# Twenty-four sums move from two vector engines to accumulating DMAs, the rounding of the angles moves to ScalarE, and the order of all steps is written anew

## The chip, the cores and the metric

The kernel runs on one core of one Trainium2 chip. The metric is the device time of one execution in microseconds (us), the median over several executions. The profile is one execution of its own, recorded by the hardware profiler.

## The reference

Three stages follow each other, with B = 4 batches, S = 768 tokens, H = 8 heads of D = 48, and so 384 channels. All inputs are fp32 on the host, but the weights arrive as float64 and are converted in the kernel.

```python
# 1. attention with a decaying state, per batch and head, over tokens t
state = alpha[t, :, None] * state + outer(k[t], v[t]);  y[t] = q[t] @ state
# 2. first block: token mixing of rank 32, then a two-layer MLP of width 1536
u  = x + (x.T @ U @ V).T;      x1 = u + relu(u @ w_ch1) @ w_ch2
# 3. second block
theta = x1 @ w_theta           # 384 x 384
zr, zi = x1 * cos(theta), x1 * sin(theta)
y = w_tok_r @ zr + w_tok_i @ zi   # 768 x 768 each, over tokens
u = x1 + y;                    out = u + relu(u @ w_ch)
```

## The kernel before, in words

Tensors lie with 128 partitions. Every large fp32 product is made from three passes of a reduced fp32 type (fp32r): each factor is split into a high part (a cast on ScalarE, L161) and a low part (source minus high part, L162, on VectorE or GpSimd), and TensorE adds hi·hi, hi·lo and lo·hi. TensorE (PE in the profile) therefore does the same number of multiplications whatever the order; VectorE (DVE), ScalarE (ACT) and GpSimd (POOL) prepare its factors.

The attention (its helpers stand at L192 to L315) scans decays on DVE (`G` L200, `al` L209), scales keys and queries on DVE or POOL (`kk` L202, `qq` L210) and multiplies on PE. The first block follows: matmuls `h` and `acc` (L545 to L547), with L566, L567 and L587 to empty their banks. `x1` is spilled to DRAM (`x1d`) and read back later into `xq`, into which the result of the mixing is added.

The second block works in 24 **theta steps**, one for a batch b and a token chunk s of 128: nine matmuls into a PSUM bank `th`, three transposes of `x1` into a bank `x1t` (L705); ACT copies `x1t` to SBUF as `xc` (L719) and so frees the bank; DVE adds and subtracts a large constant to round the angle (L721, L722); ACT takes the absolute value and two sines (L725 to L727); DVE multiplies both by `xc` (L731, twice). The results of batches 0 and 1 lie side by side in `ZR[0, s]` and `ZI[0, s]`, those of batches 2 and 3 in `ZR[1, s]` and `ZI[1, s]`, each 128x768.

The mixing treats `w_tok_r`, `w_tok_i` and the z of two halves as a product of 2x2 blocks and makes it from seven products (the order is `TERMS`) instead of eight, each summed over six chunks s. For each of the 42 pairs (product, chunk), `factors` forms sums of weights (`cv`, 128x384) and of z (128x768), all at L773, in place, and splits both factors; `products7` then issues 18 matmuls `mx` (L818), and at a product's end DVE adds the banks into `xq` (L823, L825). The split of a z waits for ACT's high part, and PE waits for both parts. `operands` splits the final u, `outputs` makes the last matmuls `ch`.

Nothing is scheduled at run time. A string `ORDER` of 876 letters gives the order in which all the generators are advanced (H is a piece of a theta step, V a half of a factor pair, G six matmuls of a product), and so the order in each engine's queue. Tables of letters (`BY_T` for the splits of weights, `BY_Z` for those of z, `BY_S` for the sums, and others) say of each operation whether it runs on POOL (P) or DVE (V). SBUF slots and the eight PSUM banks are handed out from lists, first in, first out; a step that takes a bank waits until its last reader is done. DMAs are issued from SP (SyncE).

Of the kernel before, what the change touches and what calls it, by code (L numbers as in the profile page):

```python
# [37 lines left out]
APAQPAAABUUBUBBABAUBAPBPUUABAAALAA0A0UDPP0LB0LBBAP0BB0BB1B1PAL1A2LA1L2LAA221LAL22LL1LAMLLLLMNMLLMLMNNMMLLQMMUL  # L38
MNLLNNAUQLMDML1LNLLLMNNQMNLQLLUMNLLNLNLPLMMDMPNPQMMMMMPMANABBABDBNBABQBPDABAPAABBBQBPBNBBBPNANKLKNLKADAPKKAKQP
DKLANNKKPNNKBAKDAKBBBBMABMBBPTMAMQMAPMMQPMAMM1MMKMABAMBDBLPBMQAAMBAKBBBPDKMMPAMMKMPMLKKAMMKABBABAQUAKAKQBBTDTK  # L40
NANKPLDNNNNBTLPUNKNLNLNNBAPAPBNANKN2BTNTQBKFANBKNANNKQPABBNBBBTMAKNNNKKNMNMKMKNAMMMMKMKKUTMKMAQKNMTNKKNLMKMMNX
NNNM0NNNMKTMNNNMNNNMHNMTNMHMKNNMMKMMMHHNNTHHMKMMFHFMMHMMLMNMMMHKMMHMMMHMHXTNNHMHNMHTMHTHHTTHNNVTTHTTNTNNTHXNHN
# [6 lines left out]
BY_K = "PPPPPPVPVVPPPPVP"  # L49
BY_Q = "VVPPVPPPVPVPVVVP"  # L50
BY_W = "PPPPPPPVPPPP"
BY_A = "AAAAVVAAVVAAAAVAAAVAVAAVAVVVAVVV"
BY_Z = "PPPPVVPPPPPPPPPPPPPPPPVPPPPPPVVPVPVVPVPPPP"
# [13 lines left out]
def linear_attention_moe_kernel(ctx, tc, aT, kT, qT, vP, vT, U, V4, w1, w2, wth, wtr, wti, wch, out):  # L67
# [57 lines left out]
    def two(t):  # L125
        return t.rearrange("p (a b) -> p a b", a=2)
# [12 lines left out]
    halfpi = cst.tile([128, 1], F32, name="halfpi")  # L139
    ones = cst.tile([128, 1], F32, name="ones")  # L140
# [487 lines left out]
    def load_second(whole):  # L628
# [58 lines left out]
    def theta(b):  # L687
        for hf in range(2):
# [7 lines left out]
            for q in range(3):  # L696
# [13 lines left out]
                n, xc = two(T("nn")), T("xc")[:, 0:DM]  # L710
# [15 lines left out]
                act.activation(zi, n[:, 0], ACTF.Sin, scale=NEG2PI)  # L726
                act.activation(zr, n[:, 1], ACTF.Sin, scale=NEG2PI, bias=halfpi)  # L727
# [39 lines left out]

    def factors():
# [6 lines left out]
        for p in TERMS:  # L775
            for s in range(NC):
# [5 lines left out]
                ws, w, zs, z = term(p, s)  # L782
                add(ws)
# [7 lines left out]
                WP[p, s], ZP[p, s] = t, (zh, zl)  # L791
                if p == 7:
                    done_with(ZR[1, s])
                elif p == 5:
                    done_with(ZR[0, s], WT["r", s])
                elif p == 3:
                    done_with(ZI[1, s])
                elif p == 4:
                    done_with(ZI[0, s], WT["i", s])
                yield  # L800

    def products7():
        for p in TERMS:
            for s in range(NC):
# [5 lines left out]
                for j in range(KD):  # L810
                    c = slice(j * 128, (j + 1) * 128)
                    for q in range(2):
# [391 lines left out]
```

## Time and profile before

| | |
|---|---|
| runs | 711.95, 712.21, 714.93 us; median 712.21 |
| the profiled execution | 713.35 us, its span 711.6 us |
| mean granted TensorE clock | 0.978 of full speed |
| attention and first block | to about 482 us |
| second block, while angles and factors are made | about 482 to 639 us |
| remaining products and outputs | about 639 us to the end |

The page gives busy time by engine and cuts the span into slices. Of the trace three views matter here: busy time by stretch, the chain of waits (the work that ended last, followed back), and single instructions in order of time, which show what an operation takes alone and what it takes beside another engine's.

### The profile page before, as it was taken

How to read it: one execution, taken by the hardware profiler on the slowest of the kernel's cores; microseconds unless marked ns; L12 is line 12 of the kernel's file. 1: busy time of each engine (PE TensorE's matmuls, PEld its weight loads, DVE VectorE, ACT ScalarE, POOL GpSimd, SP SyncE). 2: the span in 40 equal slices, each digit the busy share in tenths (PEclk: the TensorE clock that was granted, in tenths of full speed). 3: DMA queues.
4: the chain of work that ended last, by engine and by line, in shares of the span. 5: the costliest groups of instructions: out<-in, count | busy, mean ns of one | idle time of the engine just before them, and what ended most of it. 6: DMA issues, size and time to landing. Idle time of an engine off the chain costs nothing.

```text
span 711.6 us, 11654 instructions
## 1 busy us (share of the span) xinstructions
PE 663.9 (93%) x4658; PEld 629.5 (88%) x4658; DVE 488.1 (69%) x689; ACT 278.6 (39%) x575; POOL 240.2 (34%) x185
## 2 busy tenths in 40 slices
PE   4879999999999999999999999999897887979996
PEld 3758899888999899999999999999797876979996
DVE  8878868668556667434235438988989989984742
ACT  3444453455433534322124334445654333331410
POOL 6642326424131023000000100214567778853700
PEclk9989999999999999999999999999998999899998
DMA  8523474445423412131000102634100114002102
GB/s 318 201 93 117 168 234 147 148 115 189 165 85 117 139 46 62 35 121 57 8 39 5 63 31 83 241 134 178 45 1 1 28 62 133 1 1 77 68 23 104
DMA packets 27966, 69.10 MB, mean 97 GB/s; under 512 B 3328, under 2 KB 10368, under 8 KB 27904
## 3 DMA queue, kind: packets, MB, share of 16 engines
q1 hardware_dynamic: 27904, 68.29, 28.6%
q8 instruction: 38, 0.62, 0.3%
q14 instruction: 24, 0.20, 0.1%
HBM read 54.12 MB, written 9.44 MB: 89 GB/s over the span
## 4 chain that ended last, share of the span: by engine, by line
PE 66%; DVE 25%; issue 3%; ACT 2%; POOL 2%; DMA 1%; DVEq 0%; ACTq 0%
PE acc L545 7%; PE acc L546 7%; PE acc L547 7%; PE h L545 7%; PE h L547 6%; PE h L546 6%; PE mx L818 5%; DVE zr L773 4%; PE A L255 4%; DVE cv L773 3%; PE Y L307 2%; PE Y L315 2%; DVE xq L825 2%; PE ch L547 2%; PE ch L546 2%
## 5 line engine op out<-in xcount | busy, mean ns | idle before, releaser
L818 PE MATMUL mx<-wp,zh 128*128 128x384 f32 x504 | 135.2, 350 | 9.6 <-DVE xq L825 5.0
L567 DVE SCALAR_TENSOR_TENSOR hh<-h,hh 128x384 fp32r<-128x384 f32 x96 | 52.7, 555 | 99.4 <-ACT hh L566 99.3
L818 PEld LDWEIGHTS mx<-wp,zh 128*128 128x128 f32 x504 | 94.2, 197 | 12.0 <-ACT zh L161 3.9
L545 PE MATMUL h<-uh,wh 128*128 128x384 f32 x288 | 98.5, 342 | 1.6 <-DVE hh L567 1.6
L545 PE MATMUL acc<-hh,wh 128*128 128x384 f32 x288 | 98.4, 342 | 0.0
L546 PE MATMUL acc<-hh,wh 128*128 128x384 f32 x288 | 96.4, 335 | 1.8 <-DVE hh L567 1.8
L547 PE MATMUL h<-uh,wl 128*128 128x384 f32 x288 | 96.5, 335 | 0.0
L547 PE MATMUL acc<-hh,wl 128*128 128x384 f32 x288 | 96.5, 335 | 0.0
L546 PE MATMUL h<-uh,wh 128*128 128x384 f32 x288 | 96.4, 335 | 0.0
L818 PE MATMUL mx<-wp,zl 128*128 128x384 f32 x252 | 88.5, 351 | 7.0 <-POOL zl L162 7.0
L566 ACT ACTIVATE hh<-h 128x384 fp32r<-128x384 f32 x96 | 46.1, 490 | 101.6 <-PE h L547 98.3
L162 POOL TENSOR_TENSOR wp<-cv,wp 128x384 fp32r<-128x384 f32 x33 | 44.0, 1339 | 76.8 <-DVE zr L731 40.2
L818 PEld LDWEIGHTS mx<-wp,zl 128*128 128x128 f32 x252 | 49.8, 198 | 9.7 <-POOL zl L162 9.5
L545 PEld LDWEIGHTS h<-uh,wh 128*128 128x128 f32 x288 | 54.1, 188 | 3.5 <-DVE hh L567 2.0
L546 PEld LDWEIGHTS acc<-hh,wh 128*128 128x128 f32 x288 | 54.1, 188 | 2.0 <-DVE hh L567 2.0
L545 PEld LDWEIGHTS acc<-hh,wh 128*128 128x128 f32 x288 | 54.1, 188 | 1.2 <-ACT hh L566 0.3
L546 PEld LDWEIGHTS h<-uh,wh 128*128 128x128 f32 x288 | 54.1, 188 | 0.0
L547 PEld LDWEIGHTS acc<-hh,wl 128*128 128x128 f32 x288 | 54.1, 188 | 0.0
L547 PEld LDWEIGHTS h<-uh,wl 128*128 128x128 f32 x288 | 54.1, 188 | 0.0
L162 POOL TENSOR_TENSOR zl<-zr,zh 128x768 fp32r<-128x768 f32 x22 | 44.8, 2039 | 15.1 <-ACT zh L161 14.8
L162 POOL TENSOR_TENSOR x1s<-Y,x1s 128x384 fp32r<-128x384 f32 x9 | 11.1, 1250 | 114.4 <-ACT x1s L161 114.4
L202 POOL TENSOR_TENSOR kk<-kk,G 128x767 f32<-128x767 f32 (+1 forms) x13 | 23.2, 1787 | 52.5 <-DVE G L200 34.4
(145 smaller groups left out, 1344.9 us busy)
## 6 DMA issues: line engine op xcount, KB each, us to landing
raw<-in_w SPq DMA_DIRECT2D x12, 768.0 KB, 4.4
al<-in_aT SPq DMA_DIRECT2D x15, 384.0 KB, 3.6
kk<-in_kT SPq DMA_DIRECT2D x15, 384.0 KB, 4.2
qq<-in_qT SPq DMA_DIRECT2D x15, 384.0 KB, 5.1
vv<-in_vP SPq DMA_DIRECT2D x16, 291.0 KB, 5.5
x1d<-X SPq DMA_DIRECT2D x12, 384.0 KB, 2.9
raw<-in_wti SPq DMA_DIRECT2D x6, 768.0 KB, 4.3
raw<-in_wtr SPq DMA_DIRECT2D x6, 768.0 KB, 4.2
```

The lines of the kernel that those rows point to most:

```text
L162: (e_lo or dve).tensor_tensor(out=lo, in0=src, in1=hi.bitcast(F32), op=ALU.subtract)
L202: (dve if BY_K[b * NP + p] == "V" else pool).tensor_tensor(out=k[:, x:y - 1], in0=k[:, x:y - 1], in1=G[:, x:y - 1], op=ALU.mult)
L255: pe.matmul(ts[h][:, j * C:(j + 1) * C], k[r, c], q[r, c], start=True, stop=True)
L307: pe.matmul(t[64 * h:64 * h + n, o], v[:, c * 96 + h * D:c * 96 + h * D + n], ms[g][h][:, j], start=(j == 0), stop=(c == 0), skip_group_ch ...
L315: pe.matmul(t[64 * h:64 * h + D, o], st[64 * h:64 * h + 64, :, c - 1], q[64 * h:64 * h + 64, c * C:(c + 1) * C], start=False, stop=True, s ...
L545: pe.matmul(out, a[0], b[0], start=first, stop=False)
L546: pe.matmul(out, a[0], b[1], start=False, stop=False)
L547: pe.matmul(out, a[1], b[0], start=False, stop=last)
L566: act.activation(h[:, 0], t[:, 0:HT], ACTF.Relu)
L567: dve.scalar_tensor_tensor(out=h[:, 1], in0=t[:, 0:HT], scalar=0.0, in1=h[:, 0].bitcast(F32), op0=ALU.max, op1=ALU.subtract)
L773: (dve if next(sums) == "V" else pool).tensor_tensor(out=o, in0=x, in1=y, op=op)
L818: pe.matmul(t[:, 0:HT], x[:, q, c], w[:, y], start=f, stop=l, skip_group_check=True)
```

## The change

What it does:

- 24 of the sums of `factors` become DMAs that add their source to what lies at their destination, SBUF to SBUF, issued from POOL (`plus`). Six add the i weights' half to the r weights' (128x384, as each r weight is converted); six add `ZI[1, s]` to `ZR[1, s]` (called a here; issued when the last batch's theta step of s is written); six add that result to `ZR[0, s]` (b; `later`, after product 1's factor is split, behind a); six add `ZR[0, s]` to `ZI[0, s]` (c; after product 6's split). The signs that the other sums need come from the sines' scale and bias; product 2 is then subtracted, not added.
- The rounding's first addition goes from DVE to ACT (Identity with a bias, 24 times).
- ACT's copy of `x1t` goes (24 times). DVE's two multiplications read the PSUM bank, which is kept until they are done.
- `ORDER` and the tables are new.

Instructions in the second block up to the last weight's split (before: from the trace, 482 to 639 us; after: counted in the order of the same stretch):

| | before | after |
|---|---|---|
| DVE, two operands in SBUF, 128x384 | 57 | 40 |
| DVE, two operands in SBUF, 128x768 | 39 | 28 |
| POOL, two operands in SBUF, 128x384 | 36 | 28 |
| POOL, two operands in SBUF, 128x768 | 29 | 21 |
| POOL, accumulating DMAs | 0 | 24 |
| DVE, one operand in PSUM (`xq`, rounding, multiplications) | 58 | 69 |

TensorE's instructions are the same in number and kind; their order differs.

```diff
 ORDER = """
-APAQPAAABUUBUBBABAUBAPBPUUABAAALAA0A0UDPP0LB0LBBAP0BB0BB1B1P
...
+APQAAAPAUUBBUUBBBAAAPPBUBUUAPABAA0LD0AAAPL0BL0BABPBB00BB11PB
...
-BY_T = "PVPVPVVPVPPPPPPPPPVPPPPPPPPPPPPVPPPPPPPVPV"
-BY_S = "PVPVVVPVVVVPVVVVVVVVVVVVVVVVVVVVVVVVVPVVVVVVVVVV"
...
+BY_T = "PPPVPPPPPPVVVPVVVPVPPPVPPPPPVPVVVPVVPVVPPV"
+BY_S = "VVVVVVVVVVVVVVVVVVVVVVVVPVVVVPPVVPPVVVVPPPVVPPPP"
...
+        pool.memset(minus, -HALFPI)
+        pool.memset(magic, MAGIC)
...
-                    WT[key] = two(v)
+                    WT[key] = w = two(v)
+                    if key[0] == "r":
+                        plus(w[:, 1], WT["i", key[1]][:, 1])
...
-                n, xc = two(T("nn")), T("xc")[:, 0:DM]
+                n, xc = two(T("nn")), xt[:, 0:DM]
...
-                act.copy(xc, xt[:, 0:DM])
-                done_with(xt)
-                dve.tensor_scalar(out=n[:, 0], in0=th[:, 0:DM], scalar1=MAGIC, scalar2=None, op0=ALU.add)
+                act.activation(n[:, 0], th[:, 0:DM], ACTF.Identity, bias=magic)
...
-                act.activation(zi, n[:, 0], ACTF.Sin, scale=NEG2PI)
-                act.activation(zr, n[:, 1], ACTF.Sin, scale=NEG2PI, bias=halfpi)
+                act.activation(zi, n[:, 0], ACTF.Sin, scale=NEG2PI if b in (2, 3, "any") else -NEG2PI)
+                act.activation(zr, n[:, 1], ACTF.Sin, scale=-NEG2PI if b in (2, 3) else NEG2PI,
+                               bias=minus if b in (2, 3) else halfpi)
...
-                done_with(xc)
+                done_with(xt)
                 if b in range(B):
                     made.add((b, s))
+                    if b == B - 1:
+                        plus(ZR[1, s], ZI[1, s])
...
     def term(p, s):
-            1: ([(wr1, wr1, add, wi1)], wr0, [], b11),
-            6: ([(wr0, wr1, sub, wr0)], wr0, [(b12, b22, sub, b12), (b11, b12, add, b11)], b11),
+            1: ([], wr0, [], b11),
+            6: ([(wr0, wr1, sub, wr0)], wr0, [], b11),
...
-            5: ([], wr1, [(b21, b11, sub, b21), (b11, b22, sub, b11)], b11),
+            5: ([], wr1, [(b11, b22, sub, b11)], b11),
...
+    def plus(out, x):
+        pool.dma_start(out, x, accum_op=ALU.add)
+
+    old = []
+
+    def later(s=None):
+
+        for x in old[:]:
+            if x[1] == s or all((b, x[1]) in made for b in range(B)):
+                old.remove(x)
+                plus(*((ZR[0, x[1]], ZR[1, x[1]]) if x[0] == 1 else (ZI[0, x[1]], ZR[0, x[1]])))
...
     def factors():
+                if p in (6, 5):
+                    later(s)
...
+                later()
+                if p in (1, 6):
+                    old.append((p, s))
...
-                                if p == 4:
+                                if p in (2, 4):
                                     dve.tensor_tensor(out=x, in0=x, in1=t[:, 0:HT], op=ALU.subtract)
```

Three places in the queues show what moved. A bracket lists whom an instruction waits for; DMASW is a DMA that POOL issued, DMAHW one of SP.

First, POOL in the middle of the second block, before: splits of weights (`wp`) and of z (`zl`) with a sum between them.

```order
L773 TENSOR_TENSOR cv<-cv 128x384
L162 TENSOR_TENSOR wp<-cv,wp 128x384 [waits DVE_49,PE_49,Activation_49]
L162 TENSOR_TENSOR zl<-zr,zh 128x768 [waits Activation_49]
L162 TENSOR_TENSOR wp<-cv,wp 128x384 [waits PE_49,Activation_49]
L773 TENSOR_TENSOR zr<-zr 128x768 [waits DMAHW1_49,DVE_49]
L162 TENSOR_TENSOR zl<-zr,zh 128x768 [waits Activation_49]
```

POOL in the change, where the sums a (`zr<-zi`) and b (`zr<-zr`) are issued.

```order
L777 DMA zr<-zi 128x768 [waits DVE_49]
L166 TENSOR_TENSOR wp<-cv,wp 128x384 [waits PE_49,Activation_49]
L166 TENSOR_TENSOR zl<-zr,zh 128x768 [waits DVE_49,PE_49,Activation_49]
L777 DMA zr<-zr 128x768 [waits DMASW5_49,Pool_49]
L777 DMA zr<-zi 128x768 [waits DVE_49]
L777 DMA zr<-zi 128x768 [waits DMASW0_49,DVE_49]
L166 TENSOR_TENSOR zl<-zr,zh 128x768 [waits PE_49,Activation_49]
L777 DMA zr<-zr 128x768 [waits DMASW7_49,DMAHW2_49,DMASW1_49,Pool_49]
L777 DMA zr<-zr 128x768 [waits DMASW2_49,DMASW0_49,Pool_49]
```

The sum b waits in POOL's queue until the DMA of a has landed, and the next split stands behind it.

Second, DVE at the theta steps, before: the rounding (L721, L722) and sums (L773) of z in one queue.

```order
L721 TENSOR_SCALAR nn<-th 128x384 [waits PE_49,Pool_49]
L722 SCALAR_TENSOR_TENSOR nn<-nn,th 128x384 [waits DVE_49]
L773 TENSOR_TENSOR zr<-zi,zr 128x768
L773 TENSOR_TENSOR zr<-zr 128x768 [waits DVE_49]
L773 TENSOR_TENSOR cv<-cv 128x384
```

DVE in the change, at such a step.

```order
L726 SCALAR_TENSOR_TENSOR nn<-nn,th 128x384 [waits Activation_49,Pool_49]
L736 TENSOR_TENSOR zi<-zi,x1t 128x384 [waits PE_49,Activation_49]
L736 TENSOR_TENSOR zr<-zr,x1t 128x384 [waits Activation_49]
L726 SCALAR_TENSOR_TENSOR nn<-nn,th 128x384 [waits DVE_49,Activation_49]
L736 TENSOR_TENSOR zi<-zi,x1t 128x384 [waits PE_49,Activation_49]
```

The first rounding step and the sums of z are gone from it, and the multiplications read the bank `x1t`.

Third, PE at the transposes of a late theta step, before.

```order
L547 MATMUL th<-wt,x1s 128x384
L705 MATMUL x1t<-ident,X_2691 128x128 [waits DVE_49]
L705 MATMUL x1t<-ident,X_2904 128x128
L705 MATMUL x1t<-ident,X_3149 128x128
L818 MATMUL mx<-wp,zh 128x384 [waits Activation_49]
```

PE in the change, at two late theta steps that follow each other closely.

```order
L711 MATMUL x1t<-ident,X_2766 128x128 [waits DVE_49,PE_49]
L711 MATMUL x1t<-ident,X_2993 128x128
L711 MATMUL x1t<-ident,X_3121 128x128
L843 MATMUL mx<-wp,zh 128x384 x2
L843 MATMUL mx<-wp,zl 128x384
L843 MATMUL mx<-wp,zh 128x384 x2
L843 MATMUL mx<-wp,zl 128x384
L549 MATMUL th<-wt,x1s 128x384 [waits DVE_49]
```

In 8 of the 24 theta steps of the change the bank that `x1t` takes is the one that the `x1t` just before it held, and DVE gives it back only after its multiplications; in the order before it came back after ACT's copy.

## Rows read from the trace of the kernel before

**Rows 1.** The page's part 1: busy us, share of the span, instructions.

```profile
PE 663.9 (93%) x4658; PEld 629.5 (88%) x4658; DVE 488.1 (69%) x689; ACT 278.6 (39%) x575; POOL 240.2 (34%) x185
```

**Rows 2.** By stretch: its us; PE, PEld, DVE, ACT, POOL busy; granted clock; DMA share; GB/s.

```profile
0.00:60.00 60.00, 43.09 (x476) 35.87 (x477) 48.00 (x64) 25.09 (x56) 32.66 (x46) 0.94 0.58 200
60.00:482.00 422.00, 418.42 (x3088) 399.23 (x3087) 262.13 (x418) 169.95 (x371) 79.32 (x61) 1.00 0.32 105
482.00:540.00 58.00, 54.01 (x315) 51.76 (x313) 52.84 (x72) 33.41 (x67) 32.22 (x21) 1.00 0.19 69
540.00:639.00 99.00, 81.94 (x405) 76.51 (x404) 92.42 (x90) 34.68 (x59) 74.60 (x45) 0.90 0.13 41
640.00:700.00 60.00, 60.00 (x348) 60.00 (x347) 29.96 (x43) 14.46 (x23) 20.43 (x13) 1.00 0.17 63
```

**Rows 3.** The chain of waits from 482 to 639 us, share by engine and line.

```profile
by line: DVE zr L773 18.1%; DVE cv L773 12.5%; DVE xq L825 9.5%; issue 7.7%; DVE zr L731 5.6%; DVE zi L773 5.4%; DVE wp L162 4.4%; DVE zi L731 4.4%; DVE zl L162 4.0%; DVE nn L722 3.6%; DVE nn L721 3.6%; DVE u2l L162 3.3%; DVE cv L473 2.2%; 
```

**Rows 4.** What PE waited for, 482 to 639 us: total us, times, longest.

```profile
PE mx L818 <- POOL zl L162: 7.0, 8, 1.9
...
PE x1t L705 <- DVE nn L722: 1.1, 1, 1.1
```

**Rows 5.** In order of time, DVE and POOL at 560 us: start, duration, instruction.

```profile
560.39 0.55 DVE L773 TENSOR_TENSOR cv<-cv 128x384 f32<-128x384 f32 x1
560.86 0.94 DVE L773 TENSOR_TENSOR zr<-zi,zr 128x768 f32<-128x768 f32 x1
561.84 2.45 DVE L773 TENSOR_TENSOR zr<-zr 128x768 f32<-128x768 f32 x1
...
561.42 2.05 POOL L162 TENSOR_TENSOR zl<-zr,zh 128x768 fp32r<-128x768 f32 x1 [1.76 <-ACT zh L161]
```

**Rows 6.** Groups, 482 to 639 us: count, busy us, mean ns, idle before.

```profile
L773 DVE TENSOR_TENSOR zr<-zi,zr 128x768 f32<-128x768 f32 x11 | 22.2, 2015 | 0.2
L825 DVE TENSOR_TENSOR xq<-mx,xq 128x384 f32<-128x384 f32 x36 | 17.4, 542 | 0.0
L162 POOL TENSOR_TENSOR zl<-zr,zh 128x768 fp32r<-128x768 f32 x22 | 44.8, 2039 | 15.1 <-ACT zh L161 14.8
L162 POOL TENSOR_TENSOR wt<-cv,wt 128x384 fp32r<-128x384 f32 x3 | 3.1, 1053 | 7.2 <-ACT wt L161 7.2
```

**Rows 7.** In order of time, one theta step on DVE and ACT.

```profile
504.05 0.55 DVE L721 TENSOR_SCALAR nn<-th 128x384 f32<-128x384 f32 x1
504.63 0.55 DVE L722 SCALAR_TENSOR_TENSOR nn<-nn,th 128x384 f32<-128x384 f32 x1
...
505.22 0.53 ACT L725 ACTIVATE nn<-nn 128x384 f32<-128x384 f32 x1 [3.19 <-DVE nn L722]
...
506.70 0.56 DVE L731 TENSOR_TENSOR zr<-zr,xc 128x384 f32<-128x384 f32 x1
```

**Rows 8.** DMAs by queue (count, KB each, us to landing), and one issue on SP.

```profile
x1d<-X SPq DMA_DIRECT2D x12, 384.0 KB, 2.9
...
raw<-in_wti SPq DMA_DIRECT2D x6, 768.0 KB, 4.3
...
1.72 0.43 SPq L192 DMA_DIRECT2D qq<-in_qT  x1
```

**Rows 9.** In order of time, the attention's start on DVE and POOL.

```profile
12.05 1.76 DVE L209 TENSOR_TENSOR_SCAN al<-al,starts 128x768 f32<-128x768 f32 x1
...
24.15 1.81 POOL L202 TENSOR_TENSOR kk<-kk,G 128x767 f32<-128x767 f32 x1 [2.86 <-DVE G L200]
...
24.32 3.25 DVE L209 TENSOR_TENSOR_SCAN al<-al,starts 128x768 f32<-128x768 f32 x1
```

More of the change, by code (lines that the diff above doesn't have):

```diff
@@ L37 @@
 ORDER = """
[L38 to L42, printed above, removed]
@@ L43 @@
-NTHTHNHTTNTHTNHNVTTNTNNTHTHNNVNNTHVHGNGHTNVGVGTTXHVVGHGGGHNTVHVVGGGVGVHVTGHHGVGHHGHHGGGVVGHVHHGVGGHVHHGGHGVVGH
-VGVHHGVGGVVGGGVVGGHGGGVVHGGVGGGVGGVVVGVGVVGGVGGGGGGVVVGGGVHGVVVVGGVGVGGGGVGXVVVVXVGGGGGGVGVGVGGVVGVGGYGGGGGTTY
-GVVGGVTGGTGYVGGXGGYTGCGCCTVGCVVGGCVTCGGVGVVCGVGYCGVVCVCYGCCCGGGYYGVCCGYCCCGGVGCGCGGCYGVCGGYGTCGVCVGVCCCGYV
-"""
[L49 to L53, printed above, removed]
@@ L54 @@
-BY_X = "PVVVPPVVVPPPVVPPVPPVPVVV"
-BY_T = "PVPVPVVPVPPPPPPPPPVPPPPPPPPPPPPVPPPPPPPVPV"
-BY_U = "VVPVVVVVPVVV"
-BY_S = "PVPVVVPVVVVPVVVVVVVVVVVVVVVVVVVVVVVVVPVVVVVVVVVV"
+APQAAAPAUUBBUUBBBAAAPPBUBUUAPABAA0LD0AAAPL0BL0BABPBB00BB11PBA1LLLA122LAAA122L1ALLL22LALLLMNMLNNLMLMLLLNMLMMLNN
+MLQLLDLNQNMLMLNMMULQLDNMLQLMNLLLMMMML1NPLMUMPMPNQMANPMMNBBABDAAPABDNABBQBPABBPABBBBABBUPNABANKKLLNDKPNKKKPAKNN
+KKADAQPQNNKAKBKABBAMD1PMMLBBMLBPMBMAPMAMQBBMMMAQMBBADMABPKAQMBMAPBTDBKMBMPMMKMAKAMKAPLMAMKKLMQALABTPQBTABKKNNU
@@ new lines @@
+KKKNNBATNUNAPBNNPAPBNDNLLNNQANBAAK2NLANNQBBBNTKQBBNNATDKBAAPKNNBNBKMMTKKNNMNMABMKXKNKNKKMMKKKMMMTMFNMKNMKNHNNN
+NNNKMNMUTNNMNNMMKMMNT0NTMNNHNLHMTMKMHNHTMMMMMMMMKMHMMHMMMFKMNTHTMMTHMHHHNMHHTMNMXHNFMHHMHTTTHMTNNHNTTNNHHNNTNH
+NVTNTHXNTTVHNHHTNHTHNTNTNTNNHVTVHTNNNNHVTHVGTGTGGVVHHGXHVGGGVVVVGGGHGGTHTVHHGHHVHGVGGVGGVHGHVHVHGGHGHHVGGNVHGH
+GVGGVGGVVVHHGHGHGGGVVGVGGGVGVGGVVVVVGGGGVGVVGVGGGGGVGGGVGGGVGVGGGGVGVVVGXVVGGVGGVVGGGGGGGGGVGVGVGGXVGXVVVTYGGV
+GGGGYGVYVGGTGGVGGGCCCGYCTVTYTCVCGGCCVCGYGGGCVGYVYGVVGCCVTVGCVGVGCVCVYVCTCGCGGGVTGCCVVCGCCGVCGGCGCGGGYYYCGV
@@ L58 @@
+"""
+BY_K = "VVVPPVPPVPPPVPPV"
+BY_Q = "VVPVVPPVVPVPVVPV"
+BY_W = "PPPPPVPPPPPV"
+BY_A = "AAAAVVVAVVAVVAAAVAVAVAAVAVAAAVVV"
+BY_Z = "VPVPVPPPPPPPPPVPVPVPVPVPPVPVPVVPVPPVPVPPPV"
+BY_X = "PVVPPPVVVVPPPPPVVVVPPVVV"
+BY_T = "PPPVPPPPPPVVVPVVVPVPPPVPPPPPVPVVVPVVPVVPPV"
+BY_U = "VVPVVPPVPVPP"
+BY_S = "VVVVVVVVVVVVVVVVVVVVVVVVPVVVVPPVVPPVVVVPPPVVPPPP"
 MAGIC = 12582912.0
@@ L139, in linear_attention_moe_kernel @@
     halfpi = cst.tile([128, 1], F32, name="halfpi")
+    minus = cst.tile([128, 1], F32, name="minus")
+    magic = cst.tile([128, 1], F32, name="magic")
     ones = cst.tile([128, 1], F32, name="ones")
@@ L755, in term @@
                                   for w in (WT.get(("r", s)), WT.get(("i", s)))]
-        b11, b21, b12, b22 = ZR.get((0, s)), ZI.get((0, s)), ZR.get((1, s)), ZI.get((1, s))
-        add, sub = ALU.add, ALU.subtract
+        b11, m21, m12, b22 = ZR.get((0, s)), ZI.get((0, s)), ZR.get((1, s)), ZI.get((1, s))
+        sub = ALU.subtract
         return {
-            2: ([], wi0, [], b21),
-            1: ([(wr1, wr1, add, wi1)], wr0, [], b11),
-            6: ([(wr0, wr1, sub, wr0)], wr0, [(b12, b22, sub, b12), (b11, b12, add, b11)], b11),
-            7: ([(wi0, wi0, sub, wr0), (wr0, wi1, sub, wr0)], wr0, [], b12),
-            5: ([], wr1, [(b21, b11, sub, b21), (b11, b22, sub, b11)], b11),
+            2: ([], wi0, [], m21),
+            1: ([], wr0, [], b11),
+            6: ([(wr0, wr1, sub, wr0)], wr0, [], b11),
+            7: ([(wi0, wi0, sub, wr0), (wr0, wi1, sub, wr0)], wr0, [], m12),
+            5: ([], wr1, [(b11, b22, sub, b11)], b11),
             3: ([], wi0, [], b22),
-            4: ([], wi1, [], b21),
+            4: ([], wi1, [], m21),
         }[p]
+    def plus(out, x):
[6 more added lines that the diff above has]
+                plus(*((ZR[0, x[1]], ZR[1, x[1]]) if x[0] == 1 else (ZI[0, x[1]], ZR[0, x[1]])))
     def factors():
```

## The prediction

> **What bounds the kernel now.** I read the page's busy times first [rows 1]: PE is busy 93% of the span, so at most 7% can be won without less arithmetic. Then the table by stretch [rows 2], to see where the idle time lies. From 640 to 700 us PE runs 348 matmuls in 60 us without a gap, 0.172 us each: that is its pace when it is fed. From 60 to 482 us it is busy 418 of 422 us: nothing to win there. From 482 to 639 us it runs 315 + 405 = 720 matmuls, which at 0.172 us are 124 us, in a stretch of 157 us: 33 us are lost, 4 before 540 us and 29 after it, where the granted clock also falls to a mean of 0.90. The first 60 us hold another 17 us of PE's idle time.
>
> Who causes the 33 us? The chain of waits over this stretch [rows 3] is almost wholly DVE, led by the sums (L773: 18.1 + 12.5 + 5.4 = 36%). What PE itself waited for [rows 4] names POOL's `zl` first (7.0 us in 8 waits). Both are two sides of one thing, which the instructions in order of time show [rows 5]: a 128x384 sum takes DVE 0.55 us and a 128x768 sum 0.94 us alone, but the one that starts beside POOL's split takes 2.45 us. The groups say the same as means [rows 6]: `zr<-zi,zr` 2.02 us over 11, where the addition into `xq`, with an operand in PSUM, stays at 0.54 us. So an operation with two operands in SBUF on DVE and one on POOL take turns, and I count their times as one resource, the **pair**. DVE alone: 57 x 0.55 + 39 x 0.94 = 68 us. POOL alone, with 1.05 us for 128x384 [rows 6] and 1.81 us for 128x768 [rows 9]: 36 x 1.05 + 29 x 1.81 = 90 us. Sum 158 us in a stretch of 157 us: the pair is full, and it bounds this stretch.
>
> **The change part by part.**
>
> *Fewer operations on the pair.* After it, DVE has 40 x 0.55 + 28 x 0.94 = 48 us and POOL 28 x 1.05 + 21 x 1.81 = 67 us: 116 us, 42 us less, which is under PE's 124 us. PE becomes the bound of the stretch. It won't be fed perfectly: from 482 to 540 us, where the pair was not yet short of time, it was busy 54.0 of 58 us and ran 315 matmuls, which at 0.172 us are 54.3 us, so 1.07 times its need. 124 x 1.07 = 132 us.
>
> *The DMAs' cost on POOL.* No DMA of POOL's is in this trace. An issue costs it between 0.43 us, an issue on SP [rows 8], and 1.81 us, POOL's own operation over the same 128x768 [rows 9]: 24 issues are 10 to 43 us. I take 1 us, nearer to SP's since POOL moves no data itself: 24 us. Six sums b wait in POOL's queue for a's landing, and splits stand behind them. Landing lies between 2.9 us, a plain transfer of the same 384 KB, and 8.7 us, three times that; I take 4.3 us, that of a transfer of 768 KB [rows 8], since an addition reads both operands. In place of POOL's 1.81 us that is 2.5 us more for each b, 15 us in all. POOL then holds 67 + 24 + 15 = 106 us of 132: covered. A few splits will still come late in their place; I let two of the six waits reach PE, 5 us (0 to 15). The Trainium skill, page "DMA: Bandwidth & Descriptors", section "Anatomy of one DMA — SWDGE (gpsimd) path", fits such a transfer as 2.0 us plus the bytes over 436 thousand per us. By it 384 KB land in 2.9 us, an estimate from that page; two waits would be 2 us and not 5, and the total 3 us lower. No run here shows it yet.
>
> *The sums c and those of the weights* are used much later than they are issued (c by the products 5 and 4, the weights' by term 6): nothing, as long as a landing stays below some 7 us. For b the nearest use of its result is about seven steps of six matmuls, 7 x 6 x 0.172 = 7 us, behind its issue.
>
> *The bank `x1t`.* DVE's multiplications lie about 3.2 us behind the rounding's start [rows 7]. Where a theta step's transposes need the bank of the step before, PE waits for them unless enough products lie between: 6 matmuls are 1.0 us, 12 are 2.1 us, 9 of the next `th` another 1.6 us. Of the 8 such steps four have only 6 or 12 products between, and lose 0.5 to 2 us: I take 3 us (0 to 8). Before, this wait was 1.1 us in all [rows 4]. Reading the bank costs DVE itself nothing: 0.54 us [rows 6] against 0.56 us [rows 7].
>
> *Rounding on ACT.* 24 operations of about 0.53 us [rows 7] come to ACT and 24 copies go: even. The step's chain gains a change of engine and loses none; ACT is busy 68 of the stretch's 157 us [rows 2]. DVE is relieved of 24 x 0.55 = 13 us of the whole, 6 in this stretch, and gets none of it back. Nothing on the end: the stretch goes by PE.
>
> *The stretch:* 132 + 5 + 3 = 140 us for 157: **-17 us**.
>
> *The attention's start.* There the scan of decays takes 3.25 us beside POOL's `kk` and 1.76 us alone [rows 9]. The new tables give DVE more of the scaling (`kk` 7 of 16 for 4, `qq` 10 of 16 for 8). For pairs 2 and 3 that takes two scans from 3.25 to 1.76 us; the first pair's chain on DVE gets longer by an operation of 0.94 us [rows 5]. I take **-2 us** (-4 to +1).
>
> *The end.* From 639 us on PE is busy throughout; the last splits of u are hidden behind 27 matmuls, 4.7 us, and half of them go to POOL, where one takes 1.81 us: nothing. If that cover failed it would cost about 1 us.
>
> *Sum:* -17 - 2 = -19 us against the profiled execution's own 713.35 us, so 694.35 us. That execution stands 1.1 us above the median of the runs, 712.21 us; against the median I say **693 us**.
>
> **The rivals.**
>
> *Full gain (677 to 680 us).* PE runs the whole stretch at its pace, as from 640 us on [rows 2], because the pair now has 8 us to spare and the clock stays up. 157 - 124 = 33 us and 2 us at the start: 712 - 35 = 677 us, or 680 us with the 3 us of bank waits. For it: 640 to 700 us is without a gap. Against: even 482 to 540 us lost 7%.
>
> *The pair's time is given back as waits (705 to 716 us).* The theta steps are a chain, ACT, DVE, ACT, DVE, and the factors behind them another; if the chains and not the pair set the pace, the 42 us freed become idle time. All 8 bank waits at 2 us (16 us) or all six b waits at 2.5 us (15 us) on PE's path take the gain nearly away: 140 + 13 + 10 = 163 us where both come in full, +6, and 152 us, -5, where half of both does; with the start's -2, 705 to 716 us, middle 710. For it: PE waited for single operations of `zl` only 7 us [rows 4], so most of the loss has many small causes. Against: the sum of the pair fits the stretch within 1 us.
>
> *Slower: POOL's queue blocks (about 727 us).* If an issue holds POOL as long as its own operation did, 1.81 us, and a landing takes 12 us, POOL has 67 + 24 x 1.81 + 6 x (12 - 1.81) = 172 us, 15 us more than the stretch had: 712 + 15 = 727 us. It decides from 157 us on: 6 x (L - 1.81) = 46, a landing of L = 9.5 us with 1.81 us per issue, or 15 us with 0.43 us. For it: DVE's operations come without a break here (92 of 99 us busy [rows 2]), and if an issue takes turns with them like an operation, each also waits up to 0.94 us [rows 5]. Against: 384 and 768 KB land here in 2.9 and 4.3 us [rows 8]. The Trainium skill, page "SBUF — State Buffer", section "SBUF: two separate sides", states a rule on this side: the descriptors of a DMA issued from POOL are written by POOL itself, and while DVE holds the shared port they can't be written, so the transfer seems blocked by DVE. The rows show the turns, but no DMA of POOL's, so they bear it out by half; I give it most of this rival's chance.
>
> *The change doesn't relieve the pair at all.* If adding in a DMA cost POOL what the addition cost, the pair would stay at 116 + 43 = 159 us and the time at 712 us: this lies within the second rival.
>
> **How the numbers follow.** A measurement of this kernel can tell about 0.5%, 3.6 us, from no change. The forecast has 0.54, with a range of its own of 684 to 704 us: its terms' ends are 0 to 15, 0 to 8 and -4 to +1 us about 693. Full gain has 0.15, the second rival 0.18, the third 0.13. Faster: all of the forecast and of the full gain, and a third of the second rival (below 708.6), 0.54 + 0.15 + 0.06 = 0.75. Same: 0.08 of the second rival and 0.01 of the third. Slower: the rest, 0.16. The range from 678 to 714 us leaves out the third rival (0.13), the lowest part of the full gain (0.03) and the top of the second (0.04).
>
> **What would show it.** Right: in the changed profile the stretch from the first block's end to the last split is about 140 us with PE at 90% or more, its granted clock near 1.00, and DVE's share of the chain falls while PE's grows; `zr<-zi,zr` sums fall towards 0.94 us; POOL's issues take about 1 us, a lands in about 4 us; PE's waits at `x1t` come to 3 us and those for `zl` to no more than 7. Wrong: POOL in the chain at L777, or splits that wait for DMASW for over 5 us; PE waiting at `x1t` for over 10 us; a stretch still at 157 us with DVE and POOL both idle in it.

## The result and the profile after

The changed kernel takes 675.61 us (median of 4 runs, 675.03 to 678.09) against 712.83 us in the runs beside it: a ratio of 0.948, with a 95% interval from 0.9448 to 0.9513. The forecast was 693 us, range 678 to 714: the sign was right, the size was not, by 17 us.

The page's busy times after (us, share of the span, instructions), to be set beside [rows 1]: DVE is busy 67 us less, ACT as before, and PE is at 96%.

```profile
PE 649.3 (96%) x4658; PEld 620.5 (92%) x4658; DVE 420.7 (62%) x667; ACT 279.9 (42%) x573; POOL 215.1 (32%) x185
```

By stretch after (columns as in [rows 2]). The first block now ends at 471.1 us, not at 482.1; the last matmuls `ch` begin at 601.6 us, not at 636.9, and PE ends at 667.3 us, not at 705.4.

```profile
0.00:60.00 60.00, 46.51 (x535) 38.74 (x537) 52.59 (x81) 26.45 (x61) 27.16 (x42) 1.00 0.61 213
60.00:471.00 411.00, 410.86 (x3026) 393.43 (x3023) 241.27 (x397) 169.64 (x365) 73.20 (x63) 1.00 0.32 106
471.00:540.00 69.00, 65.55 (x384) 63.70 (x383) 44.33 (x76) 42.36 (x81) 45.27 (x38) 1.00 0.61 137
540.00:602.00 62.00, 61.05 (x348) 59.70 (x347) 50.51 (x68) 24.90 (x42) 41.40 (x29) 1.00 0.43 108
602.00:662.00 60.00, 60.00 (x348) 59.98 (x347) 29.80 (x44) 16.57 (x26) 28.03 (x16) 1.00 0.18 63
```

So the 38.1 us by which PE ends earlier come from three places: 11.0 up to the end of the first block, 24.3 from there to the first `ch` (154.8 to 130.5 us), 2.8 after it (68.5 to 65.7 us). From 471 to 602 us PE runs 384 + 348 = 732 matmuls, 126.2 us at 0.1724 us, in 131 us: 4.8 us are lost where 33 were. The granted clock is 1.00 in every row. Before it was 0.90 from 540 to 639 us [rows 2]: 405 matmuls needed 69.8 us there and kept PE busy for 81.9, so 12 us of the 29 lost in that stretch were matmuls that took longer, up to 10 of them by the clock (a tenth of 99 us), and 17 us were idleness.

What PE waits for in that stretch (total us, times, longest), beside [rows 4]: the bank `x1t` costs 0.6 us, the splits `zl` 0.5 us.

```profile
PE th L549 <- DVE nn L726: 2.8, 1, 2.8
PE x1t L711 <- DVE zr L736: 0.6, 2, 0.3
PE mx L843 <- POOL zl L166: 0.5, 1, 0.5
PE mx L843 <- DVE xq L850: 0.4, 1, 0.4
```

The DMAs that POOL issued, by kind (count, KB each, median us to landing), beside [rows 8]. The last two lines are the same view of two short windows, 506 to 507 us and 540 to 544 us:

```profile
zr<-zi POOLq DMA_DIRECT2D x6, 384.0 KB, 6.2
zr<-zr POOLq DMA_DIRECT2D x6, 384.0 KB, 4.0
zi<-zr POOLq DMA_DIRECT2D x6, 384.0 KB, 8.6
...
cv<-cv POOLq DMA_DIRECT2D x6, 192.0 KB, 5.2
...
zr<-zi POOLq DMA_DIRECT2D x1, 384.0 KB, 4.0
...
zi<-zr POOLq DMA_DIRECT2D x4, 384.0 KB, 9.4
```

The first `zr<-zi`, with no other transfer of POOL's or SP's in flight, landed in 4.0 us; four `zi<-zr` issued within 3.5 us, with reads of SP's in flight too, landed in 7.5 to 11.4 us.

Groups on DVE and POOL from 471 to 602 us (columns as in [rows 6]). The record of an issue lasts 0.87 to 1.49 us in the mean. The sums that stayed on DVE take 1.24 us in the mean, for 2.02 us before; the multiplications from the bank take 0.55 us.

```profile
L793 DVE TENSOR_TENSOR zr<-zi,zr 128x768 f32<-128x768 f32 x6 | 7.3, 1242 | 0.0
...
L736 DVE TENSOR_TENSOR zi<-zi,x1t 128x384 f32<-128x384 f32 x11 | 6.1, 554 | 9.3 <-ACT zi L730 8.0 <-PE mx L843 1.0
...
L726 DVE SCALAR_TENSOR_TENSOR nn<-nn,th 128x384 f32<-128x384 f32 x11 | 6.1, 553 | 11.3 <-ACT nn L725 11.3
```

```profile
L777 POOL DMA_DIRECT2D zi<-zr x6 | 7.0, 1493 | 0.0
L777 POOL DMA_DIRECT2D zr<-zi x6 | 6.5, 1080 | 0.8 <-DVE zr L736 0.5 <-PE mx L843 0.2
L777 POOL DMA_DIRECT2D zr<-zr x6 | 5.2, 871 | 8.5 <-DMA zr<-zi 4.5 <-issue 4.0
```

The longer records begin before the record of POOL's instruction ahead of them has ended, and are longer by that overlap. Without it an issue lasts 0.86 to 0.88 us (the first one 1.02), whether DVE is idle or busy. At 549.65 us, for one, it takes 0.86 us beside a split on DVE:

```profile
548.18 2.34 DVE L166 TENSOR_TENSOR zl<-zr,zh 128x768 fp32r<-128x768 f32 x1 [0.18 <-ACT zh L165]
...
549.65 0.86 POOL L777 DMA_DIRECT2D zi<-zr  x1
```

The chain of waits over the same stretch is now half PE, and DVE has left its head. It also shows landings:

```profile
by line: PE mx L843 49.1%; DMA zr<-zi 11.9%; DMA xq<-x1d 7.6%; issue 4.4%; DMA zr<-zr 3.1%; POOL zr L777 2.8%; POOL zl L166 2.3%; PE th L551 2.0%; PE th L549 2.0%; PE th L550 2.0%; DVE zl L166 1.4%; DVE nn L726 1.3%; ACT nn L725 1.3%; ACT n
```

Read alone, its 12 + 3% of landings (20 us) would be taken for a cost. Run 14 below shows that they cost nothing: the chain names one path, and a share in it is not yet a price.

### The profile page after: what moved, and what is told of

It is laid out like the page before. It is cut to its first block, busy times and chain, and to the rows that moved or that the text cites. A ratio compares the mean times of both kernels' runs of the same rounds, so it can differ in the third digit from the quotient of the medians.

```text
span 673.8 us, 11687 instructions
## 1 busy us (share of the span) xinstructions
PE 649.3 (96%) x4658; PEld 620.5 (92%) x4658; DVE 420.7 (62%) x667; ACT 279.9 (42%) x573; POOL 215.1 (32%) x185
## 4 chain that ended last, share of the span: by engine, by line
PE 84%; DMA 5%; DVE 4%; POOL 2%; ACT 2%; issue 1%; SPq 0%; DVEq 0%; ACTq 0%; POOLq 0%
PE mx L843 14%; PE acc L549 8%; PE h L549 8%; PE acc L551 7%; PE h L550 7%; PE h L551 7%; PE acc L550 7%; PE A L259 4%; PE Y L311 3%; DMA zr<-zi 2%; PE Y L319 2%; PE ch L549 2%; PE ch L550 2%; PE ch L551 2%; PE D L290 2%; DMA xq<-x1d 1%
## 5 line engine op out<-in xcount | busy, mean ns | idle before, releaser
L843 PE MATMUL mx<-wp,zh 128*128 128x384 f32 x504 | 129.5, 337 | 0.4 <-DVE xq L850 0.4
L843 PEld LDWEIGHTS mx<-wp,zh 128*128 128x128 f32 x504 | 90.2, 188 | 1.5 <-DVE xq L850 0.9
L843 PE MATMUL mx<-wp,zl 128*128 128x384 f32 x252 | 84.4, 335 | 0.5 <-POOL zl L166 0.5
L843 PEld LDWEIGHTS mx<-wp,zl 128*128 128x128 f32 x252 | 47.3, 188 | 0.9 <-POOL zl L166 0.9
L266 POOL TENSOR_SCALAR_AFFINE_SELECT Am<-Am 128x384 f32<-128x384 f32 x34 | 24.1, 735 | 53.5 <-ACT Am L265 53.5
L166 POOL TENSOR_TENSOR wp<-cv,wp 128x384 fp32r<-128x384 f32 x24 | 30.4, 1270 | 26.4 <-ACT wp L165 22.0
L166 POOL TENSOR_TENSOR zl<-zr,zh 128x768 fp32r<-128x768 f32 x16 | 33.5, 2094 | 7.1 <-ACT zh L165 7.1
```

What stands on the lines that cost most here:

```text
L166: (e_lo or dve).tensor_tensor(out=lo, in0=src, in1=hi.bitcast(F32), op=ALU.subtract)
L266: pool.affine_select(out=m, in_=m, pattern=[[0, 3], [1, C]], compare_op=ALU.is_ge, fill=0.0, base=0, channel_multiplier=-1)
L843: pe.matmul(t[:, 0:HT], x[:, q, c], w[:, y], start=f, stop=l, skip_group_check=True)
```

## The experiments

Two times of each run are compared below: its median, and from its trace the **second block's time**, from the first block's end to PE's last matmul: 223.3 us before, 196.2 us after. A ratio is to the runs of the kernel before that were taken beside it, with its interval.

### The code and the order, one without the other

Run 1 takes the new code with the old order and tables:

```diff
-ORDER, BY_K, BY_Q, BY_W, BY_A, BY_X, BY_Z, BY_T, BY_U of the change
+ORDER, BY_K, BY_Q, BY_W, BY_A, BY_X, BY_Z, BY_T, BY_U of before
```

> The changed code (accumulating DMAs, rounding on ACT, x1 read from its bank) run in the order and with the tables of the kernel before. Theory 'pair' (operations with two SBUF operands on DVE and on POOL take turns, and their sum bounded the second block): in the second block's 157 us the sum falls from 158 to about 123 us as in the change, so that stretch goes by PE and gains 17 to 27 us, while the start gains nothing: 686 to 696 us. Rival 'order' (what won is the new order of the steps, not fewer operations): 708 to 713 us.

Measured: 712.87 us (ratio 1.0012, 0.9996 to 1.0028); the second block takes 221.4 us. Run 2 takes the old code with the new order:

```diff
-ORDER and all tables of before
+ORDER and all tables of the change
-xc = T("xc")[:, 0:DM]
+xc = pools["sml"].tile([128, DM], F32, tag="xc", name="xc", bufs=2)
```

> The code of the kernel before (sums as DVE and POOL operations, rounding on DVE, ACT's copy xc kept, in a small buffer of its own) run in the new order with the new tables. Theory 'pair': the pair's sum in the second block is about 164 us again, so the block takes some 157 us or more as before, and only the start's 11 us stay: 698 to 706 us. Rival 'order': about 675 to 682 us.

Measured: 713.44 us (1.0013, 1.0004 to 1.0023). Its first block ends at 471.4 us, as in the change, so the start's 11 us belong to the order and the tables; its second block takes 234.0 us, 10.7 us more than before. Neither theory holds: in the second block the code alone gains 2 us, the order alone loses 11, and both together gain 27. Run 2 is a rough measure of the order, though: the old code has 48 sums for the letters of `BY_S`, of which the change reads only the first 24, and the other 24 put 12 sums on POOL, where the order before had 5. In run 2, from 471.4 to 639.7 us, DVE is busy 122.6 of 168.3 us and waits for the rest, mostly for ACT (38 us); before, it was busy 145 of 157 us [rows 2]. In run 1, at 540 to 580 us, the chain of waits says what the old order does to the new code:

```profile
by line: DMA zr<-zi 28.3%; POOL zl L166 17.4%; issue 11.0%; POOL wp L166 11.0%; DMA zr<-zr 9.8%; DVE cv L793 5.4%; DVE wp L166 4.8%; PE mx L843 3.9%; POOL zi L777 3.4%; DVE xq L850 2.9%; ACT wp L165 1.3%; POOL zr L777 1.2%; POOLq L166 0.3%;
```

The order of POOL's instructions there shows how (start, duration, idle before): b is held in POOL's queue until a has landed, 5.4 us, and the next splits stand behind it.

```profile
562.24 1.47 POOL L777 DMA_DIRECT2D zr<-zi  x1
569.08 0.86 POOL L777 DMA_DIRECT2D zr<-zr  x1 [5.37 <-DMA zr<-zi]
569.62 1.21 POOL L777 DMA_DIRECT2D zi<-zr  x1
570.18 1.67 POOL L166 TENSOR_TENSOR wp<-cv,wp 128x384 fp32r<-128x384 f32 x1
574.05 3.91 POOL L166 TENSOR_TENSOR zl<-zr,zh 128x768 fp32r<-128x768 f32 x2 [2.21 <-ACT zh L165]
```

ACT waits too: its cast `zh` needs the sum b. What ACT and POOL waited for landings from 470 to 640 us (total us, times, longest), first in run 1, then in the change:

```profile
ACT zh L165 <- DMA zr<-zr: 17.9, 2, 13.2
POOL zr L777 <- DMA zr<-zi: 11.6, 4, 5.4
```

```profile
ACT zh L165 <- DMA zr<-zr: 1.6, 1, 1.6
POOL zr L777 <- DMA zr<-zi: 4.5, 2, 2.9
```

### What the DMAs cost in either order

Run 13, in the old order, and run 14, in the new one, leave the sums out:

```diff
     def plus(out, x):
-        pool.dma_start(out, x, accum_op=ALU.add)
+        return
```

> The changed code in the old order with the old tables, its 24 accumulating DMAs left out altogether: the products work on z and weights that were not summed, so this part of the computation is missing. With the DMAs it takes 712.9 us. Theory 'landings' (the old order loses to the landings of the sums what DVE and POOL gained): without them the block gains 15 to 25 us, 688 to 698 us. Rival 'letters' (the old order feeds PE badly whatever DVE and POOL have to do): 704 us or more.

Measured: 690.14 us (0.9675, 0.9649 to 0.9702), 22.7 us less than run 1; the second block takes 201.0 us. By stretch (columns as in [rows 2]) from 540 to 580 us, first run 1, then this one:

```profile
540.00:580.00 40.00, 28.91 (x138) 26.85 (x138) 22.22 (x23) 9.11 (x16) 28.76 (x25) 0.84 0.66 132
```

```profile
540.00:580.00 40.00, 39.40 (x225) 38.48 (x224) 34.98 (x37) 17.42 (x30) 32.06 (x21) 1.00 0.31 99
```

With the DMAs PE runs 138 matmuls in these 40 us at a clock of 0.84, without them 225 at 1.00. So the old order would have used the freed engines well; the DMAs took it all back.

> The changed kernel with its 24 accumulating DMAs left out altogether (the same part of the computation is missing). Theory 'landings are hidden in the new order': issues, waits and landings together cost no more than 2 us there, 673 to 676 us. Rival 'they cost what I forecast' (5 us of waits that reach PE, and issues on POOL): 666 to 671 us.

Measured: 676.23 us (0.9476, 0.9453 to 0.9498), against 675.61 us with the DMAs: in the new order all 24 together cost nothing that can be measured. So the DMAs cost 23 us in one order and 0 in the other. Both runs leave out issues as well as landings. But the number of issues is the same in both orders, and what differs is the waiting for landings, 29.5 us on ACT and POOL against 6.1 us in the lines above.

Run 11 replaces the old order's DMAs by DVE operations:

```diff
-        pool.dma_start(out, x, accum_op=ALU.add)
+        dve.tensor_tensor(out=out, in0=out, in1=x, op=ALU.add)
```

> The changed code in the old order with the old tables (as in the first run of this study, 712.9 us), its 24 DMAs replaced by DVE additions: 20 us more on DVE, but nothing lands late. Theory 'landings': the old order lost to DMA landings what the freed engines gained; without them 698 to 708 us. Rival 'engine load': DVE gets busier, 714 us or more.

Measured: 707.36 us, 5.5 us less than with DMAs. The additions took DVE 31 us there, not 20 (a 128x768 one 1.54 to 1.61 us in the mean by kind), and still cost less than 24 transfers that are off DVE and POOL but late.

### The sums back on an engine, in the new order

Run 3 puts them on POOL:

```diff
-        pool.dma_start(out, x, accum_op=ALU.add)
+        pool.tensor_tensor(out=out, in0=out, in1=x, op=ALU.add)
```

> The changed kernel with its 24 accumulating DMAs replaced by POOL additions in the same places. Theory 'pair': 6 x 1.05 + 18 x 1.81 = 39 us come back to the pair, 116 + 39 = 155 us against PE's 124: the second block gets 15 to 25 us longer, 690 to 700 us. Rival 'engines apart' (each engine counts for itself): POOL then has 67 + 39 = 106 us, below PE's 124, and saves 24 issues: 675 to 680 us.

Measured: 696.75 us (0.9788, 0.9771 to 0.9804), 21 us slower than the change. Run 4 has `dve` in place of `pool`:

> The changed kernel with its 24 accumulating DMAs replaced by DVE additions in the same places. Theory 'pair': 6 x 0.55 + 18 x 0.94 = 20 us come back, 116 + 20 = 136 us, a little over what PE needs: 3 to 10 us slower, 679 to 686 us, clearly less than with the sums on POOL. Rival 'DVE alone is the bound': 88 + 20 = 108 us on DVE, below 124: 674 to 678 us. If instead the DMAs' issues and waits cost something on PE's path, this kernel is faster than the change.

Measured: 693.56 us (0.9739, 0.9722 to 0.9756), 18 us slower. Both theories of run 4 missed. The sums on POOL do cost far more than POOL's own load explains, but by the traces the 23 us that the sums took on DVE cost nearly as much as the 45 us that they took on POOL: the pair's sum doesn't give the price.

### Taking turns, or DVE's time?

Runs 5 and 6 add needless operations to DVE's queue at the same places. They were meant to take the same time, in run 5 with operands in SBUF, in run 6 without:

```diff
     def plus(out, x):
         pool.dma_start(out, x, accum_op=ALU.add)
+        if x.free_size() == 768:
+            for _ in range(2):
+                dve.tensor_tensor(out=scr[:, 0:573], in0=scr[:, 0:573], in1=scr[:, 0:573], op=ALU.add)
```

(the other one: `dve.memset(scr, 0.0)`, 128x768.)

> The changed kernel with two needless DVE additions (two operands in SBUF, 128x573, by width 0.70 us each) on a scratch tile behind each of the 18 z sums' DMAs: 36 x 0.70 = 25 us on DVE, read by nobody. Theory 'pair': the pair gets 116 + 25 = 141 us plus the DMAs' issues, as loaded as with the sums on DVE: 15 to 25 us slower than the change, 690 to 700 us. Rival 'DVE time': only DVE's own time counts, 88 + 25 = 113 us; then it is the same as the run with memsets, whatever that is.

Measured: 705.93 us, 30.3 us slower than the change.

> The same with 36 memsets of 128x768 (0.70 us each in the trace of before) in place of the additions: the same time in DVE's queue, but no operand read from SBUF. Theory 'pair': 676 to 682 us, at least 8 us less than with the additions. Rival 'DVE time': the two runs agree within 3 us.

Measured: 701.27 us, 25.7 us slower. The groups of the needless operations, first the additions, then the memsets (count, busy us, mean ns, idle before):

```profile
L782 DVE TENSOR_TENSOR scr<-scr 128x573 f32<-128x573 f32 x36 | 36.8, 1023 | 0.7
```

```profile
L782 DVE MEMSET scr<- 128x768 f32 x36 | 25.1, 698 | 6.4 <-DVE scr L782 4.8
```

The additions do take turns with POOL: alone one takes 0.75 us (not 0.70), and six that met an operation of POOL's took 2.05 to 2.93 us. The memsets wait for one another, 4.8 us in all. From one start to the next, the additions fill 36.9 us of DVE's queue and the memsets 29.0, so 8 us more of queue are worth 4.7 us of the end. Neither theory's range was met (at least 8 us apart for the pair, within 3 us for DVE's time). But memsets, which read nothing from SBUF, should have cost next to nothing if the pair alone were the bound. Counted from the traces, a two-operand operation on DVE or any operation on POOL runs in 104 of the 156 us that this stretch takes with the memsets, and in 107 of 131 us in the change. So the pair alone is not what bounds the new order. It may well have bounded the kernel before: there the same count is 142 of 157 us, and no run tests it there.

What the added work meets is the order in DVE's queue. PE's longest wait is for DVE's rounding in a late theta step. In the change it takes 2.8 us (above); with the additions and then with the memsets (total us, times, longest):

```profile
PE th L551 <- DVE nn L728: 12.2, 2, 11.0
```

```profile
PE th L551 <- DVE nn L728: 7.5, 1, 7.5
```

With the sums on DVE (run 4) the longest such wait is 9.7 us, with the sums on POOL (run 3) 5.9 us. With work added to DVE or POOL the long wait begins at 529 to 533 us, where the theta steps end. By stretch from 532 to 562 us (columns as in [rows 2]). First the change, then the additions, then the memsets:

```profile
532.00:562.00 30.00, 29.08 (x165) 28.21 (x164) 22.94 (x37) 11.67 (x19) 21.20 (x18) 1.00 0.93 206
```

```profile
532.00:562.00 30.00, 16.91 (x75) 16.20 (x74) 24.64 (x32) 7.70 (x15) 14.73 (x13) 0.72 0.60 109
```

```profile
532.00:562.00 30.00, 19.07 (x86) 17.73 (x85) 21.65 (x37) 8.56 (x17) 13.52 (x13) 0.77 0.68 125
```

PE falls from 165 matmuls to 75 and 86, and where it idles the mean granted clock is 0.72 and 0.77, so that what it does run is slower as well: the loss grows beyond its cause. For the whole stretch, first the change, then the memsets:

```profile
471.00:602.00 131.00, 126.60 (x730) 123.39 (x729) 94.84 (x143) 67.25 (x123) 86.67 (x66) 1.00 0.53 123
```

```profile
471.70:627.50 155.80, 136.26 (x726) 130.32 (x725) 119.29 (x179) 66.58 (x123) 85.71 (x66) 0.92 0.45 104
```

Of the 25 us that it gets longer with the memsets, 15 are idleness of PE and 10 are slower matmuls at a clock of 0.92. That 25 us of memsets cost 25.7 us is therefore chance, not a price of one for one.

### The two smaller edits

Run 7 puts the rounding back:

```diff
-                act.activation(n[:, 0], th[:, 0:DM], ACTF.Identity, bias=magic)
+                dve.tensor_scalar(out=n[:, 0], in0=th[:, 0:DM], scalar1=MAGIC, scalar2=None, op0=ALU.add)
```

> The changed kernel with only the rounding's first addition back on DVE (24 operations from PSUM, 11 in the second block's stretch, 6 us). Theory 'pair': they don't read two operands from SBUF, so the pair is as it was: 674 to 679 us. Rival 'DVE's queue': each theta step stands 0.55 us longer in a queue that everything shares: 680 us or more.

Measured: 675.05 us, the same as the change. DVE's 10 waits for ACT at L726, 11.3 us in the group above, go with it, and DVE has room for the 6 us. Run 12 does the same on top of the sums on DVE:

> The changed kernel with both the 24 sums and the rounding's first addition on DVE (the sums alone gave 693.6 us). Theory 'DVE's queue' (what counts is its busy time and its waits for ACT in the theta steps together): the rounding on DVE takes away a wait of about 1.2 us for an operation of 0.55 us per step, 11 times: 685 to 692 us. Rival 'DVE's busy time': 11 x 0.55 = 6 us more: 697 to 701 us.

Measured: 698.29 us, 4.7 us more than with the sums alone, as the rival said. My theory of waits and busy time as one sum is wrong: where DVE has no room, 6 us of its busy time in the stretch cost 4.7 us, and the waits for ACT that went with them gave nothing back.

Run 8 keeps ACT's copy:

```diff
+                act.copy(xc, xt[:, 0:DM])
+                done_with(xt)
```

> The changed kernel with ACT's copy of x1t back (in a small buffer of its own) and the multiplications reading it: 22 operations of the stretch have two operands in SBUF again. Theory 'pair': 22 x 0.55 = 12 us more, 128 us without the issues; by what the sums on DVE cost (18 us for 20 us of load) that is 8 to 13 us: 683 to 689 us. Rival 'bank': the early return of the bank x1t is worth more than that, up to the 3 us that I gave it: 672 to 677 us.

Measured: 679.24 us, 3.6 us slower, between the two ranges. With the copy, the two multiplications of a step take DVE 0.95 and 0.66 us in the mean, from the bank 0.55 us each. Reading the bank, without ACT's copy and with the bank's late return, is worth 3.6 us net; the run does not take the three apart.

### The start

Run 9 restores two tables of before, run 10 the string `ORDER`:

```diff
-BY_K, BY_Q of the change
+BY_K, BY_Q of before
```

> The changed kernel with only the tables of the attention's scaling (kk, qq: POOL or DVE) of the kernel before. In the change the first block ends 11.0 us earlier (471.1 for 482.1 us). Theory 'tables': the scaling on POOL, which makes the scans on DVE wait, is what held the start; 8 to 11 us come back, 683 to 687 us, with PE's waits for kk and qq near the 15 us of before. Rival 'letters': the new order of the letters gives PE other work during these waits; 675 to 678 us.

Measured: 678.32 us; the first block ends at 475.1 us: 4.0 of the 11.0 us are the tables'. (In three runs with the old order and tables it ends at 480.4 to 483.0 us, so a us or two says nothing.)

```diff
-ORDER of the change
+ORDER of before
```

> The changed code with the old string of letters but all the new tables. For the start, theory 'tables': the first block ends 8 to 11 us earlier than before, at 471 to 474 us; rival 'letters': at 479 to 482 us. For the second block, theory 'landings' (the old letters issue a sum's DMA just ahead of its use, so DMA landings of 4 to 6.5 us stand in the chain): the block and the rest stay near 221 us, 693 to 703 us in all if the tables help the start, 709 to 713 us if not. Rival 'tables' for the second block too: near 196 to 200 us, 671 to 690 us in all.

Measured: 713.2 us; the first block ends at 477.6 us, and the second takes 225.6 us. Again the tables give about 4 us of the start, and the letters the other 7. In its first 60 us PE runs 535 matmuls after, for 476 before [rows 2]; how the letters bring their part was not taken apart. In the second block the tables alone give nothing. With the old tables that was the DMAs' doing (above); with these it wasn't tried without the sums, but ACT and POOL wait 11.4 and 10.8 us for landings of b and a there too. What PE waited for in the first 60 us, before and then after, in part:

```profile
PE kT L275 <- POOL kk L202: 9.3, 4, 5.3
PE A L255 <- POOL qq L210: 6.0, 2, 3.0
```

```profile
PE kT L279 <- DVE starts L212: 5.1, 1, 5.1
PE D L290 <- ACT kt L280: 3.5, 2, 2.1
PE A L259 <- POOL qq L214: 2.0, 1, 2.0
```

No run of the study is clearly faster than the change.

## Why the prediction was wrong, point by point

Two terms of the sum failed. The attention's start was put at -2 us and gave -11.0: 9 us of the miss. The stretch was put at 140 us and took 130.5: it gave -24.3 us where I had -17. The end, put at nothing, gave -2.8. The sign and the place of the gain in the second block were right.

- *What bounds the kernel.* That 33 us were lost in the second block, and that DVE and POOL lost them, was right. That the sum of their two-operand times is the one bound is not shown. It matched the stretch within 1 us, and the trace agrees that the pair was nearly full before (142 of 157 us). But in the new order memsets outside that sum cost 25.7 us (run 6), and the price of the sums on DVE and on POOL does not follow it (runs 3 and 4). DVE's own 145 of 157 us [rows 2] are no simpler answer, since they hold what POOL added: alone, its operations are 68 + 58 x 0.55 = 100 us.
- *"124 x 1.07 = 132 us".* The factor came from 482 to 540 us of before, which I took for a stretch that is not short of anything; it was nearly as full of DVE as the next (52.8 of 58 us [rows 2]). After, it is 131 / 126 = 1.04, waits included. I also had not taken apart the 29 us: up to 10 of them were the clock of 0.90, and came back by themselves once PE was fed.
- *"Two of the six waits reach PE, 5 us".* An issue takes 0.87 us for my 1 us, and a's landing 4.0 us alone, as I took it (4.3), but 6.2 us at the median, with others in flight. POOL waited 8.5 us ahead of the sums b, for my 15. None of it costs anything at the end: in the new order ACT waits only 1.6 us for a landing of b, in the old one 17.9 us. By the Trainium skill, page "DMA: Bandwidth & Descriptors", section "Anatomy of one DMA — SWDGE (gpsimd) path", 384 KB land in 2.9 us, an estimate from that page's fit; the trace has medians of 4.0 to 8.6 us, so the measurement decides, and it does not agree.
- *The bank `x1t`, 3 us.* Measured 0.6 us. The mechanism is there, the term was too large; reading the bank gained 3.6 us net, which I had put at nothing beyond the pair's sum.
- *Rounding on ACT, nothing.* Right here (no measurable difference when undone), and 4.7 us where DVE has no room.
- *The attention's start, -2 us.* It was -11.0 us: the largest error of the sum. I read the two tables, which give 4 us, and priced two scans; I didn't follow the new string, which gives 7, on PE in the first 100 us, where PE starts its 700th matmul at 88.6 us for 97.1. The table of stretches had told me that 17 us were idle there.
- *The sum.* -19 us had -2 and -17; measured are -11.0, -24.3 and -2.8. The end belongs to the order: from the first `ch` on PE takes 65.7 to 65.8 us in every kernel with the new order and 67.8 to 70.4 us in those with the old. The rival "full gain" (677 to 680 us) came within 2 us by luck: it had 33 us for the stretch and 2 for the start. My own range of 684 to 704 us did not follow from its terms either, whose ends add up to 683 and 711.
- *The slower rival.* POOL's queue behind DMAs did not block in this order. In the old order the DMAs take away 22.7 us, by ACT's waits for b as much as by POOL's for a. The rule of the Trainium skill, page "SBUF — State Buffer", section "SBUF: two separate sides", that POOL can't write a DMA's descriptors while a DVE operation of a certain mode holds the port that they share, is not seen here, and I had taken it for any DVE operation on that port: without an overlap with POOL's own instruction ahead, an issue took 0.86 to 0.88 us with DVE idle and with DVE busy (the first one 1.02), and leaving all of them out changed nothing.

## What to carry to other kernels

A sum moved to a DMA trades busy time for landing time. Here that was free in the order in which ACT and POOL hardly waited for landings, and cost all that it had gained in the order in which they did: the code without its order (712.9 us) and the order without its code (713.4 us) looked worthless, together they were worth 37 us. So cost a new order by following the waiting engines through it, not by the tables alone, and count with a landing of 4 us alone and up to 11 us with others in flight. To tell contention from plain load, put equal times into the same queue with and without the contended operands, and read from the trace what time they really took.

## What the runs showed that was not expected

- Adding DMAs of 384 KB, SBUF to SBUF, landed in 4.0 to 8.6 us (medians by kind), against 3.4 us for plain 384 KB to DRAM and 4.5 to 5.5 us from DRAM in the same profile. Their landing grew with the number in flight, from 4.0 us to 11.4 us. An issue took POOL 0.87 us, and where POOL's next instruction had nothing to wait for it began about 0.6 us after the issue's start.
- The granted clock turns a shortage into a larger one: from 532 to 562 us it was 1.00 where PE was fed and 0.72 to 0.77 where it idled for 36 to 44% of the time.
- An operation with two operands in SBUF takes turns with one on POOL (0.75 us alone, 2.05 to 2.93 us beside it in run 5), yet 8 us more of DVE's queue by such turns cost 4.7 us of the end, while 29 us of plain memsets cost 25.7 us, 10 of them by slower matmuls. Why waits for ACT on the same queue could be removed for nothing (run 12) while memsets could not be added for nothing stays open.
